# Feature weights loaded first through GpSimd's queue, with K and Q alone on the two hardware queues

## The chip, the cores and the metric

The kernel runs on one core of a Trainium2 chip. The metric is device time in microseconds of one execution. A core has five engines with lists of their own: TensorE (PE; its weight loads are listed apart as PEld), VectorE (DVE), ScalarE (ACT), GpSimd (POOL) and SyncE (SP). Three of them issue transfers here, each on its own queue: SP and ScalarE on hardware queues, GpSimd on a queue whose transfers can also change the number type. 16 DMA engines carry all of them.

## The reference

Two layers follow each other. The first is linear attention with a feature map: K and Q, 8 batches of 8 heads of 576 tokens of 64 numbers, are multiplied by one 64 x 128 matrix `w_phi`, and the features are exponentials of the result and of its negative.

```python
def phi(x):
    proj = np.einsum('bhsd,df->bhsf', x, w_phi)
    proj = proj - np.max(np.abs(proj), axis=-1, keepdims=True)
    return np.concatenate([np.exp(proj), np.exp(-proj)], axis=-1)
q_p, k_p = (phi(q), phi(k))
kv = np.einsum('bhsf,bhsd->bhfd', k_p, v)
z = np.sum(k_p, axis=2)
num = np.einsum('bhsf,bhfd->bhsd', q_p, kv)
den = np.einsum('bhsf,bhf->bhs', q_p, z)[..., None] + 1e-06
return (num / den).astype(np.float32)
```

The second takes the heads side by side as 512 channels, forms a gate by a causal convolution over 5 tokens and a sigmoid, multiplies it with `x @ w_val`, and multiplies by `w_out`. The result is 8 x 576 x 512 in float32.

## The kernel before

The work is cut into 40 units. Units 0 to 31 hold two heads each (four units to a batch) and eight of each token group's nine tokens; units 32 to 39 hold the ninth tokens of a batch. For each unit TensorE transposes K and Q (step T), a copy brings the transposes to SBUF (C), TensorE multiplies them with the weights (PK for K by token, PA and PQ for Q), VectorE takes maxima (MA, MB, MQ), ScalarE takes exponentials (KA, KB, XA, XB), GpSimd scales V (V), and TensorE forms kv (KV) and the output (N). The second layer follows batch by batch (GF, TH, VA, VB, GV, OA, OB, OE, ST).

The order of all this is a list written out by hand, `ORDER` (lines 31 to 108). A token names a step, its unit, after @ the PSUM banks, and after a colon the engine. Each engine and each queue carries out its part in this order; where data come from another engine or a transfer it waits, and all that stands behind it on the same engine waits too.

Ahead of the list stands an opening that the list doesn't govern (lines 157 to 238). GpSimd makes the identity `ident_bf` (line 158). The first two heads of K and of Q come in float32 to the staging buffers `first["k"]` and `first["q"]` (shown as GV, whose memory they borrow), half through SP's queue and half through ScalarE's (lines 189 and 195). The weights come to `wtmp` twice, to the upper and the lower 64 partitions (line 193), between K and Q on the same two queues. VectorE clears buffers and derives a negative identity and two small ones from `ident_bf` (lines 203 to 233). Everything else of K, Q and V comes through GpSimd's queue, which changes it to bf16 on the way, by the steps LD of the list.

The list then begins like this:

```python
LD.0 LD.1 CQ.0:D Z.1:P CK.0:A T.0@5 LD.3 LD.2 W.0:A C.0:A PK.0@0,2 KA.0 TX.0@7 CX.0:A MB.0 T.1@1 C.1:D
PA.0@6,7 PK.1@1,3 KB.0 KB.1 PQ.0@2,4 MQ.0 MA.1 SA.0 MB.1 KA.1 MA.0 T.2@5 C.2:D T.3@3 XA.0 WB.0:P C.3:D
T.32@0,1 C.32:D PA.3@6,7 XB.0 LD.4 PK.32@0,1 E.0 LD.6 LD.7 LD.5 FL.6@4 PK.2@5,2:W K0.32 K1.32 MQ.3 MB.2 KA.2
```

CK.0 and CQ.0 cast the first K (ScalarE) and Q (VectorE) to bf16. T.0 transposes that K and TX.0 that Q, C.0 and CX.0 copy the transposes, both on ScalarE. W.0 casts the weights to `W2` on ScalarE, between CK.0 and C.0; WB.0 casts them to the zero-padded `W2Z` on GpSimd. LD.0 and LD.1 load heads 2 and 3 of batch 0 of K and Q, which T.1 reads; LD.2 and LD.3 load its other four heads, which T.2 and T.3 read. LD.4 and LD.5 load V of batch 0, LD.6 and LD.7 K and Q of batch 1, the first reader of which is T.4.

Of the kernel before, what the change touches and what calls it, by code (L numbers as in the profile page):

```python
# [10 lines left out]
ALU = mybir.AluOpType  # L11
AX = mybir.AxisListType

FP32 = mybir.dt.float32
# [3 lines left out]
F = 128  # L18
DM = 512
P = 128  # L20
# [95 lines left out]
def kernel(  # L116
# [11 lines left out]
    nc = tc.nc  # L128
    ctx.enter_context(nc.allow_low_precision("bf16 operands of the matmuls"))

    def pool(name, bufs):
        return ctx.enter_context(tc.tile_pool(name=name, bufs=bufs))

    const = pool("const", 1)
# [19 lines left out]

    ctx.enter_context(tc.manual_schedule())

    ident_bf = const.tile([P, P], BF16, name="ident_bf")
    make_identity(nc, ident_bf[:])

# [28 lines left out]
        first[name] = first[name].rearrange("p (a j d) -> p a j d", a=1, d=D)  # L188
    main_dma((nc.sync, nc.scalar), "k", 0, 0, 1, first["k"])
    W2 = const.tile([P, F], BF16, name="W2")  # L190
    wtmp = const.tile([P, F], FP32, name="wtmp")
    for t in range(2):
        (nc.sync, nc.scalar)[t].dma_start(wtmp[t * 64:(t + 1) * 64, :], w_phi[:, :])
    for t in range(2):
        (nc.sync, nc.scalar)[t].dma_start(
            first["q"][t * 64:(t + 1) * 64, 0, :, :].rearrange("p j d -> p (j d)"),
# [4 lines left out]
    nident = const.tile([P, P], BF16, name="nident")  # L201
# [3 lines left out]
    nc.scalar.activation(warm[:, :], zero[:, 0:1], AF.Exp)  # L205
    W2Z = const.tile([P, 2, F], BF16, name="W2Z")
    nc.vector.memset(W2Z[:, :, :].rearrange("p a f -> p (a f)"), 0.0)
    nc.vector.tensor_scalar_mul(nident[:, :], ident_bf[:, :], -1.0)
    ident5 = const.tile([5, 5], FP32, name="ident5")
    nc.vector.tensor_copy(ident5[:, :], ident_bf[0:5, 0:5])  # L210
    id32 = const.tile([P, 32], FP32, name="id32")
    nc.vector.tensor_tensor(id32[:, :], ident_bf[:, 0:32], ident_bf[:, 32:64], ALU.add)
    nc.vector.tensor_tensor(id32[:, :], id32[:, :], ident_bf[:, 64:96], ALU.add)
    nc.vector.tensor_tensor(id32[:, :], id32[:, :], ident_bf[:, 96:128], ALU.add)

    XTs = []
    for i in range(2):
        t = const.tile([P, HP, (4 + J) * 64], BF16, name=f"XT{i}")
# [12 lines left out]
    MQA = const.tile([P, 40, 4, 2], BF16, name="MQA")  # L231
    MQX = const.tile([P, NG, P], BF16, name="MQX")
    nc.vector.memset(MQX[:, :, :].rearrange("p g c -> p (g c)"), 0.0)
    MQT = const.tile([P, NG, P], BF16, name="MQT")
    EA = const.tile([P, 40, 2, 4, 2], FP32, name="EA")
    RCPA = const.tile([P, 40, 8], FP32, name="RCPA")
# [3 lines left out]
    def copy(eng, dst, x, bank=()):  # L240
        if eng == "A":
            read(nc.scalar.activation(dst, x, AF.Copy), bank)  # L242
        else:
            read(engines[eng].tensor_copy(dst, x), bank)  # L244
# [317 lines left out]
    def op_MC(i, eng):  # L562
        x, bank = units[i].MT
        copy(eng, MQT[:, i // G % NG, :], x, bank)

# [91 lines left out]
    def op_SA(i):  # L657
        u = units[i]
        for blk in range(2 if u.tail else 4):
            for par in range(2):  # L660
# [3 lines left out]
                else:  # L664
                    r = slice(par * 64, par * 64 + 64)
                    c = par * 64 + i % G * 4 + blk
                    lhs, rhs = nident[r, c:c + 1].to_broadcast([64, P]), MQT[r, i // G % NG, :]
                nc.tensor.matmul(cols, lhs, rhs, start=False, stop=True, skip_group_check=True)  # L668
# [260 lines left out]
    for token in ORDER.split():  # L929
        head, _, eng = token.partition(":")  # L930
        head, _, bank = head.partition("@")
        name, _, idx = head.partition(".")
# [39 lines left out]
```

## Time and profile before

| | us |
|---|---|
| median of 3 runs | 225.01 |
| lowest and highest | 224.21, 226.33 |
| the profiled execution's own time | 226.87 |
| its span, first to last instruction | 225.1 |
| transfers of GpSimd's queue (q0), share of the 16 DMA engines' span | 47.6% |

In the profile a row of the timeline gives the start in us, the duration, the engine, the line, the operation, what it writes and reads, and in brackets the engine's idle time before it and what ended that. A row of transfers gives what is loaded, the queue that issues it, its size and the microseconds from issue to landing. Line numbers are those of the kernel before; line 178 issues K and V, 172 Q on GpSimd's queue, 193 the weights, 195 the first Q; 242 and 244 are the helper `copy` on ScalarE and on the other engines; 393 is a transpose and 443 a product with the weights.

### The profile page before, as it was taken

The numbers are of one execution on the slowest core, as the hardware profiler recorded it, in microseconds if no ns is written. First come the engines' busy times: TensorE is split into PE (matmuls) and PEld (weight loads), VectorE is DVE, ScalarE is ACT, GpSimd is POOL, SyncE is SP. The second block draws the span as 40 slices with busy tenths as digits, with TensorE's granted clock in tenths as the row PEclk, the third lists the DMA queues.
The fourth block names the chain that finished last, engine by engine and source line by source line (L and its number), as shares of the span: only waits on it lengthen the run. The fifth ranks groups of instructions, "written<-read, shape, count | busy, mean of one in ns | idle before, by whom it ended". The sixth has DMA issues, their size and how long they took to land.

```text
span 225.1 us, 8971 instructions
## 1 busy us (share of the span) xinstructions
PE 202.4 (90%) x3828; PEld 138.2 (61%) x3854; DVE 184.1 (82%) x337; ACT 194.4 (86%) x425; POOL 133.4 (59%) x172
## 2 busy tenths in 40 slices
PE   0687899996798999999998999999999999999997
PEld 0464677765465665678656775776676666466542
DVE  6499999987886999889996999999988997466341
ACT  3599999998988998999998999999989998777541
POOL 8779967999779702993359509952816086500100
PEclk9997999999999999999999999999999999999999
DMA  5999997699999996984928595796550226304846
GB/s 114 197 199 218 270 203 116 121 204 173 132 167 205 152 147 142 179 141 55 197 50 115 62 203 111 169 136 111 126 114 20 57 47 129 134 4 114 247 105 192
DMA packets 41362, 31.38 MB, mean 139 GB/s; under 512 B 16869, under 2 KB 37349, under 8 KB 41322
## 3 DMA queue, kind: packets, MB, share of 16 engines
q0 software_dynamic: 20816, 14.90, 47.6%
q1 hardware_dynamic: 19882, 15.04, 29.9%
q10 hardware_dynamic: 624, 0.87, 1.2%
q8 instruction: 30, 0.49, 0.9%
q14 instruction: 10, 0.08, 0.1%
HBM read 32.58 MB, written 9.44 MB: 187 GB/s over the span
## 4 chain that ended last, share of the span: by engine, by line
PE 57%; ACT 26%; DVE 9%; issue 3%; DMA 2%; SPq 1%; ACTq 0%; DVEq 0%
PE PS L841 11%; PE PS L812 10%; ACT QT L551 9%; ACT KT L538 8%; PE PS L443 5%; PE PS L706 5%; PE PS L629 4%; PE PS L393 4%; ACT GATE L801 3%; PE PS L652 3%; PE PS L785 3%; PE PS L668 2%; DMA GV<-in_q_dram 2%; DVE MKA L509 2%; PE PS L288 2%
## 5 line engine op out<-in xcount | busy, mean ns | idle before, releaser
L615 POOL TENSOR_TENSOR VT<-vN,EA 128x1024 bf16<-128x1024 bf16 x32 | 61.0, 1907 | 37.2 <-ACT EA L569 30.8
L538 ACT ACTIVATE KT<-PS 128x512 bf16<-128x512 f32 x128 | 70.7, 659 | 2.3 <-PE PS L443 2.2
L551 ACT ACTIVATE QT<-PS 128x512 bf16<-128x512 f32 x128 | 69.2, 657 | 2.8 <-PE PS L668 2.5
L509 DVE TENSOR_REDUCE MKA<-PS 128x4 f32<-128x512 f32 x64 | 42.6, 682 | 1.6 <-ACT KT L538 0.8
L494 DVE TENSOR_REDUCE MQX<-PS 128x8 bf16<-128x1024 f32 x30 | 36.5, 1219 | 4.7 <-PE PS L443 4.4
L812 PE MATMUL PS<-XT,WVAL 128*128 128x512 bf16 x128 | 34.8, 380 | 0.1
L841 PE MATMUL PS<-WOUT,GV 128*128 128x512 bf16 x107 | 30.9, 380 | 1.3 <-issue 0.6
L443 PE MATMUL PS<-W,T 64*128 64x128 bf16 x472 | 24.5, 223 | 4.3 <-ACT T L242 1.8
L828 DVE SCALAR_TENSOR_TENSOR GV<-GATE,PS 128x512 bf16<-128x512 bf16 x32 | 20.9, 680 | 5.3 <-PE PS L812 5.3
L443 PEld LDWEIGHTS <-T 64*128 64x128 bf16 x472 | 15.9, 96 | 12.9 <-issue 6.6
L726 DVE TENSOR_TENSOR XN<-PS,RCPA 128x512 bf16<-128x512 f32 x32 | 22.1, 692 | 1.1
L606 POOL TENSOR_TENSOR VTZ<-vN,EA 64x512 bf16<-64x512 bf16 x16 | 16.6, 1040 | 10.3 <-PE PS L668 6.5
L629 PEld LDWEIGHTS <-KT 128*128 128x128 bf16 x512 | 18.6, 97 | 6.6 <-ACT QT L551 1.2
L629 PE MATMUL PS<-VT,KT 128*128 128x65 bf16 x512 | 21.0, 193 | 1.5 <-ACT QT L551 0.6
L244 POOL COPY XT<-XT 128x1008 bf16<-128x1008 bf16 x8 | 8.2, 1025 | 22.3 <-ACT XT L242 16.1
L706 PEld LDWEIGHTS <-QT 128*128 128x128 bf16 x512 | 18.6, 97 | 4.3 <-issue 0.4
L706 PE MATMUL PS<-KVSA,QT 128*128 128x65 bf16 x512 | 20.6, 193 | 0.1
L244 DVE COPY T<-PS 128x1024 bf16<-128x1024 bf16 x27 | 18.3, 683 | 1.6 <-PE PS L393 1.6
L393 PE MATMUL PS<-ident_bf,kN 128*128 128x128 bf16 x128 | 13.5, 233 | 6.1 <-ACT kN L242 5.5
L801 ACT ACTIVATE GATE<-PS 128x1024 bf16<-128x1024 f32 x16 | 16.0, 1082 | 3.4 <-PE PS L785 3.4
L812 PEld LDWEIGHTS <-WVAL 128*128 128x128 bf16 x128 | 10.5, 97 | 8.4 <-issue 0.6
L852 DVE TENSOR_SCALAR OS<-PS 128x512 f32<-128x512 f32 x16 | 10.9, 685 | 5.5 <-PE PS L841 5.5
(103 smaller groups left out, 371.1 us busy)
## 6 DMA issues: line engine op xcount, KB each, us to landing
out_dram<-OS SPq DMA_DIRECT2D x28, 256.0 KB, 3.6
kN<-in_k_dram POOLq DMA_DIRECT2D x14, 320.0 KB, 7.1
vN<-in_v_dram POOLq DMA_DIRECT2D x14, 320.0 KB, 5.9
qN<-in_q_dram POOLq DMA_DIRECT2D x7, 576.0 KB, 10.8
OS<-in_moe_w_val_dram SPq DMA_DIRECT2D x1, 1024.0 KB, 9.4
out_dram<-OSt SPq DMA_DIRECT2D x8, 128.0 KB, 2.4
vN<-in_v_dram POOLq DMA_DIRECT2D x4, 160.0 KB, 8.0
OS<-in_moe_w_out_dram SPq DMA_DIRECT2D x2, 256.0 KB, 4.4
```

The costliest lines, as they stand in the source:

```text
L244: read(engines[eng].tensor_copy(dst, x), bank)
L443: nc.tensor.matmul(PS[:, bank[par], c0 + blk * P:c0 + (blk + 1) * P], u.T[r, i, blk, :], W2[r, :], start=True, stop=True,)
L494: read(nc.vector.tensor_reduce(MQX[:, i // G % NG, :].rearrange("p (r c) -> p r c", r=2)[:, :, c:c + 4], tokview(u.PA, 0, u, None), AX.X, ...
L509: read(nc.vector.tensor_reduce(out, half_ps(bank, x, out, wide), AX.X, ALU.max, apply_absolute_value=True,), [bank[x]])
L538: read(nc.scalar.activation(out, half_ps(u.PK, x, out, u.PKwide), AF.Exp, scale=1.0 if ft == 0 else -1.0,), [u.PK[x]])
L551: read(nc.scalar.activation(dst, PS[:, u.PQ[x], :].rearrange("p (x t) -> p x t", t=64), AF.Exp, scale=1.0 if ft == 0 else -1.0,), [u.PQ[x]])
L615: e.tensor_tensor(u.VT[:, :, :, 0:D], x.unsqueeze(1).to_broadcast([P, 2, n, D]), w.unsqueeze(3).to_broadcast([P, 2, n, D]), ALU.mult,)
L629: nc.tensor.matmul(PS[:, bank[0], c:c + E1], u.KT[:, ft, j // 2, j % 2, :], u.VT[:, ft, j, :], start=(jj == 0 and x == 0), stop=False, ski ...
L706: nc.tensor.matmul(PS[:, bank[c // 2], x * E1:(x + 1) * E1], u.QT[:, ft, c, h2, :, :].rearrange("p j t -> p (j t)"), kv[:, ft, h2, :], sta ...
L801: read(nc.scalar.activation(m.GATE[q2][:, :, :], banks(*bank), AF.Tanh), bank)
L812: nc.tensor.matmul(PS[:, m.val[jt], :], WVAL[:, dt, jt * P:(jt + 1) * P], planes(xt(m.b), slice(0, P), dt, 4), start=(dt == 0), stop=(dt = ...
L841: nc.tensor.matmul(PS[:, bank, :], lhs(jt), WOUT[:, jt, :], start=(jt == 0), stop=(jt == 3))
```

## The change

The two transfers of the weights leave SP's and ScalarE's queues, and are issued by GpSimd ahead of the identity. The five instructions of VectorE that read the identity move behind its clears. The hand-written list is the same.

```diff
     ctx.enter_context(tc.manual_schedule())
 
+    wtmp = const.tile([P, F], FP32, name="wtmp")
+    for t in range(2):
+        nc.gpsimd.dma_start(wtmp[t * 64:(t + 1) * 64, :], w_phi[:, :])
     ident_bf = const.tile([P, P], BF16, name="ident_bf")
     make_identity(nc, ident_bf[:])
...
     W2 = const.tile([P, F], BF16, name="W2")
-    wtmp = const.tile([P, F], FP32, name="wtmp")
-    for t in range(2):
-        (nc.sync, nc.scalar)[t].dma_start(wtmp[t * 64:(t + 1) * 64, :], w_phi[:, :])
     for t in range(2):
         (nc.sync, nc.scalar)[t].dma_start(
...
     nc.vector.memset(W2Z[:, :, :].rearrange("p a f -> p (a f)"), 0.0)
-    nc.vector.tensor_scalar_mul(nident[:, :], ident_bf[:, :], -1.0)
-    ident5 = const.tile([5, 5], FP32, name="ident5")
-    nc.vector.tensor_copy(ident5[:, :], ident_bf[0:5, 0:5])
-    id32 = const.tile([P, 32], FP32, name="id32")
-    nc.vector.tensor_tensor(id32[:, :], ident_bf[:, 0:32], ident_bf[:, 32:64], ALU.add)
-    nc.vector.tensor_tensor(id32[:, :], id32[:, :], ident_bf[:, 64:96], ALU.add)
-    nc.vector.tensor_tensor(id32[:, :], id32[:, :], ident_bf[:, 96:128], ALU.add)
...
     nc.vector.memset(MQX[:, :, :].rearrange("p g c -> p (g c)"), 0.0)
+    nc.vector.tensor_scalar_mul(nident[:, :], ident_bf[:, :], -1.0)
+    ident5 = const.tile([5, 5], FP32, name="ident5")
+    nc.vector.tensor_copy(ident5[:, :], ident_bf[0:5, 0:5])
+    id32 = const.tile([P, 32], FP32, name="id32")
+    nc.vector.tensor_tensor(id32[:, :], ident_bf[:, 0:32], ident_bf[:, 32:64], ALU.add)
+    nc.vector.tensor_tensor(id32[:, :], id32[:, :], ident_bf[:, 64:96], ALU.add)
+    nc.vector.tensor_tensor(id32[:, :], id32[:, :], ident_bf[:, 96:128], ALU.add)
```

GpSimd's list before, from the identity to the first load of V. The rows at lines 178 and 172 are LD.0, LD.1, LD.3 and LD.2, then come the two casts of WB.0 and LD.4; DMASW and DMAHW are semaphores of transfers of GpSimd's and of the hardware queues:

```order
masks.py:197 MEMSET ident_bf 128x128
masks.py:199 ISA
masks.py:199 AFFINE_SELECT ident_bf<-ident_bf 128x128 [waits Pool_49]
L178 DMA kN<-in_k_dram 64x2x320 x2
L172 DMA qN<-in_q_dram 128x576
L334 MEMSET OS 128x1
L172 DMA qN<-in_q_dram 128x2x576
L178 DMA kN<-in_k_dram 64x4x320 x2
L244 CAST W2Z<-wtmp 64x128 [waits DMAHW3_49,DVE_49]
L244 CAST W2Z<-wtmp 64x128 [waits DMAHW2_49,Pool_49]
L178 DMA vN<-in_v_dram 64x4x320 x2
```

The same place now (the line numbers of the changed kernel are a few higher or lower):

```order
L159 DMA wtmp<-in_w_phi_dram 64x128 x2
masks.py:197 MEMSET ident_bf 128x128
masks.py:199 ISA
masks.py:199 AFFINE_SELECT ident_bf<-ident_bf 128x128 [waits Pool_49]
L181 DMA kN<-in_k_dram 64x2x320 x2
L175 DMA qN<-in_q_dram 128x576
L333 MEMSET OS 128x1
L175 DMA qN<-in_q_dram 128x2x576
L181 DMA kN<-in_k_dram 64x4x320 x2
L243 CAST W2Z<-wtmp 64x128 [waits DMASW0_49,DVE_49]
L243 CAST W2Z<-wtmp 64x128 [waits DMASW1_49,Pool_49]
L181 DMA vN<-in_v_dram 64x4x320 x2
```

Two issues stand ahead of the identity and of every load of this queue, and the casts of WB.0 wait for transfers of the same queue. The order behind is the same.

ScalarE's list before, from its first issue to C.0 (the third row is the issue of the first Q, the last four are CK.0, W.0, C.0 and the first exponential):

```order
L178 DMA GV<-in_k_dram 64x2x320
L193 DMA wtmp<-in_w_phi_dram 64x128
L195 DMA GV<-in_q_dram 64x576
L205 ACT_TABLE_LOAD
L205 ACTIVATE warm<-zero 128x1 [waits DVE_49]
L242 ACTIVATE kN<-GV 128x640 [waits DMAHW1_49,DMAHW0_49]
L242 ACTIVATE W_109<-wtmp 128x128 [waits DMAHW3_49,DMAHW2_49]
L242 ACTIVATE T<-PS 128x512 [waits PE_49]
L538 ACTIVATE KT<-PS 128x4x128 [waits PE_49]
```

The same place now:

```order
L181 DMA GV<-in_k_dram 64x2x320
L195 DMA GV<-in_q_dram 64x576
L205 ACT_TABLE_LOAD
L205 ACTIVATE warm<-zero 128x1 [waits DVE_49]
L241 ACTIVATE kN<-GV 128x640 [waits DMAHW1_49,DMAHW0_49]
L241 ACTIVATE W_112<-wtmp 128x128 [waits DMASW1_49,DMASW0_49]
L241 ACTIVATE T<-PS 128x512 [waits PE_49]
L537 ACTIVATE KT<-PS 128x4x128 [waits PE_49]
```

One issue less stands between K and Q (SP's list loses the same row), and W.0 waits for GpSimd's queue.

VectorE's list before, from the second clear to CQ.0 (XT, DIAGF, VTZ and MQX are clears):

```order
L207 MEMSET W2Z 128x128
L208 TENSOR_SCALAR nident<-ident_bf 128x128 [waits Pool_49]
L210 CAST ident_124<-ident_bf 5x5
L212 TENSOR_TENSOR id_126<-ident_bf 128x32
L213 TENSOR_TENSOR id_126<-id_126,ident_bf 128x32 [waits DVE_49]
L214 TENSOR_TENSOR id_126<-id_126,ident_bf 128x32 [waits DVE_49]
L219 MEMSET XT_130 128x4x4
L219 MEMSET XT_132 128x4x4
L227 MEMSET DIAGF 128x1280
L229 MEMSET VTZ_140 128x1040
L233 MEMSET MQX 128x256
L244 CAST qN<-GV 128x576 [waits DMAHW5_49,DMAHW4_49]
```

The same place now:

```order
L207 MEMSET W2Z 128x128
L211 MEMSET XT_123 128x4x4
L211 MEMSET XT_125 128x4x4
L219 MEMSET DIAGF 128x1280
L221 MEMSET VTZ_133 128x1040
L225 MEMSET MQX 128x256
L226 TENSOR_SCALAR nident<-ident_bf 128x128 [waits Pool_49]
L228 CAST ident_141<-ident_bf 5x5
L230 TENSOR_TENSOR id_143<-ident_bf 128x32
L231 TENSOR_TENSOR id_143<-id_143,ident_bf 128x32 [waits DVE_49]
L232 TENSOR_TENSOR id_143<-id_143,ident_bf 128x32 [waits DVE_49]
L243 CAST qN<-GV 128x576 [waits DMAHW3_49,DMAHW2_49]
```

The wait for the identity stands behind all clears, and CQ.0 still comes behind the same twelve instructions.

## The prediction

> **What bounds the kernel now.** I read the page first, then the chain of work that ended last in order of time, then the timeline of the first 14 us, and last the transfers issued in short windows of it.
>
> ```profile
> span 225.1 us, 8971 instructions
> PE 202.4 (90%) x3828; PEld 138.2 (61%) x3854; DVE 184.1 (82%) x337; ACT 194.4 (86%) x425; POOL 133.4 (59%) x172
> PE 57%; ACT 26%; DVE 9%; issue 3%; DMA 2%; SPq 1%; ACTq 0%; DVEq 0%
> ...
> 2.42 5.33 DMA GV<-in_q_dram
> 8.37 1.48 PE PS L393 x12
> 9.87 0.70 DVE T L244
> ```
>
> TensorE, ScalarE and VectorE are each busy over 80% of the span, and the chain is compute from 8.37 us to the end. Only its head is a transfer: the 5.33 us in which the first head pair of Q came in. What the change can move directly is therefore the opening, and what it gains there lasts only if no later transfer gives it back. The opening, with the start in us first, then the duration, and the idle time of the engine and its releaser in brackets:
>
> ```profile
> 1.44 1.37 POOL L178 DMA_DIRECT2D kN<-in_k_dram  x2
> 2.80 0.58 POOL L172 DMA_DIRECT2D qN<-in_q_dram  x1
> 3.41 0.73 POOL L172 DMA_DIRECT2D qN<-in_q_dram  x1
> 4.11 1.28 POOL L178 DMA_DIRECT2D kN<-in_k_dram  x2
> 4.67 0.74 ACT L242 ACTIVATE kN<-GV 128x640 bf16<-128x640 f32 x1 [0.38 <-DMA GV<-in_k_dram]
> 5.46 0.61 PE L393 MATMUL PS<-ident_bf,kN 128*128 128x128 bf16 x4 [5.46 <-ACT kN L242]
> 6.71 0.31 ACT L242 ACTIVATE W<-wtmp 128x128 bf16<-128x128 f32 x1 [1.30 <-DMA wtmp<-in_w_phi_dram]
> 6.76 0.63 POOL L244 CAST W2Z<-wtmp 64x128 bf16<-64x128 f32 x2 [1.37 <-DMA wtmp<-in_w_phi_dram]
> 6.92 0.58 ACT L242 ACTIVATE T<-PS 128x512 bf16<-128x512 bf16 x1
> 7.34 1.24 POOL L178 DMA_DIRECT2D vN<-in_v_dram  x2
> 7.55 0.61 PE L443 MATMUL PS<-W,T 64*128 64x128 bf16 x8 [1.49 <-ACT T L242]
> 7.85 0.46 DVE L244 CAST qN<-GV 128x576 bf16<-128x576 f32 x1 [2.88 <-DMA GV<-in_q_dram]
> 8.66 0.47 PEld L393 LDWEIGHTS <-kN 128*128 128x128 bf16 x4
> 9.09 0.47 PEld L393 LDWEIGHTS <-qN 128*128 128x128 bf16 x4
> 9.17 0.61 ACT L242 ACTIVATE T<-PS 128x512 bf16<-128x512 bf16 x1
> 9.82 0.34 PEld L443 LDWEIGHTS <-T 64*128 64x128 bf16 x8 [0.26 <-ACT T L242]
> 9.89 0.82 POOL L172 DMA_DIRECT2D qN<-in_q_dram  x1
> 10.48 1.23 DVE L478 TENSOR_REDUCE MQA<-PS 128x8 bf16<-128x1024 f32 x1
> 12.48 0.47 PEld L393 LDWEIGHTS <-kN 128*128 128x128 bf16 x4
> 21.03 0.47 PEld L393 LDWEIGHTS <-qN 128*128 128x128 bf16 x4
> ```
>
> Two waits for transfers stand here. ScalarE casts the feature weights (W.0, 6.71) after 1.30 us idle, and the copy behind it (C.0, 6.92) has been ready since TensorE ended T.0 at 5.46 + 0.61 = 6.07. VectorE casts Q (CQ.0, 7.85) after 2.88 us idle. The rows at 8.66 and 9.09 are T.1, the first step that reads the loads of GpSimd's queue; 12.48 is T.2; 21.03 is the Q half of T.4. When each transfer landed follows from rows of short windows (the last figure is us from issue to landing; the first row is what all queues moved in 40 slices of 12 us):
>
> ```profile
> GB/s 0 0 0 0 0 0 0 60 124 260 391 304 201 185 76 86 119 188 174 189 201 245 246 192 209 192 165 201 198 206 199 193 192 192 179 181 192 188 179 188
> GV<-in_k_dram SPq DMA_DIRECT2D x1, 160.0 KB, 3.8
> GV<-in_k_dram ACTq DMA_DIRECT2D x1, 160.0 KB, 3.2
> GV<-in_q_dram ACTq DMA_DIRECT2D x1, 144.0 KB, 5.4
> GV<-in_q_dram SPq DMA_DIRECT2D x1, 144.0 KB, 5.3
> wtmp<-in_w_phi_dram ACTq DMA_DIRECT2D x1, 32.0 KB, 3.4
> wtmp<-in_w_phi_dram SPq DMA_DIRECT2D x1, 32.0 KB, 5.1
> ...
> kN<-in_k_dram POOLq DMA_DIRECT2D x1, 80.0 KB, 3.6
> kN<-in_k_dram POOLq DMA_DIRECT2D x1, 80.0 KB, 5.9
> qN<-in_q_dram POOLq DMA_DIRECT2D x1, 144.0 KB, 5.8
> qN<-in_q_dram POOLq DMA_DIRECT2D x1, 288.0 KB, 6.6
> kN<-in_k_dram POOLq DMA_DIRECT2D x1, 160.0 KB, 6.9
> qN<-in_q_dram POOLq DMA_DIRECT2D x1, 576.0 KB, 10.8
> ```
>
> On GpSimd's queue the two pieces of LD.0 landed at 1.44 + 3.6 = 5.0 and about 2.1 + 5.9 = 8.0 (the second is issued half way through the 1.37 us), LD.1 at 2.80 + 5.8 = 8.6, LD.3 at 3.41 + 6.6 = 10.0, the last of LD.2 at about 4.75 + 6.9 = 11.65, and LD.7 at 9.89 + 10.8 = 20.7. The rate falls to 76 and 86 GB/s near 4.2 to 4.8 us, just where the weights' small pieces pass the two hardware queues, and is about 190 once GpSimd's queue runs alone.
>
> **The change part by part.**
>
> Added on GpSimd: two weight issues ahead of everything. No row has this transfer on this queue. The nearest is the pair of LD.0, also from 64 partitions: 1.37 us. The bounds are two of the shortest issue (2 x 0.58 = 1.16) and two of the longest (2 x 0.82 = 1.64). I take 1.37. The identity and LD.0, LD.1, LD.3, LD.2 all move back by that. TensorE first needs the identity at 5.46, so that part is free. The loads' issue now ends at 4.11 + 1.28 + 1.37 = 6.76, and GpSimd stood idle 1.37 us before its casts at 6.76, so from there its list, with LD.4 at 7.34 and all later loads, stays where it was. The cost of this part is only that four early loads are issued 1.37 us later; it falls on T.1 and T.2, below.
>
> Where the weights land: issued at about 0.74 and 1.4, where SP and ScalarE issue K now. With 3.6 us (LD.0's first piece, alone at the head of this queue, as the weights will be) the second lands at 5.0; with 5.9 at 7.3. Before, the later half landed at 1.55 + 5.1 = 6.65. I take 5.0, by the row whose place in the queue is the same. ScalarE is ready for W.0 at 4.67 + 0.74 = 5.41, so its 1.30 us of waiting goes.
>
> Removed on SP and ScalarE: the weights' issues, behind K and ahead of Q. K keeps its issue; beside it 64 KB of weights now run on a third queue instead of behind it. Bounds for K's later half: from 0.6 earlier (the other half landed 3.2 after issue, not 3.8) to 0.2 later (64 KB at the 304 to 391 GB/s of K's own slices). I take no move, so CK.0 stays at 4.67.
>
> ScalarE's path then is: CK.0 to 5.41, W.0 to 5.72 inside TensorE's T.0, and C.0 once T.0 ends: 6.07, plus 0.08 of handover, makes 6.15 instead of 6.92. That is **0.77 us**, and PK.0 (7.55), CX.0 (9.17), PA.0 (9.82) and the reduction MQ.0 (10.48) hang on it one after another.
>
> Q: its two issues come earlier by the removed ones, to about 1.5 us on both queues. With the same 5.4 us to landing Q is there at 6.9 instead of 7.7, and CQ.0 starts at about 7.0 instead of 7.85: 0.85 us, a little more than the other path, and so no bound. If Q were as fast as K it would be there at 5.3, and nothing more would come of that, since TX.0 stands behind PK.0 in TensorE's list.
>
> The clears: the same twelve instructions of VectorE in another order; the five on the identity go last, which keeps VectorE from waiting for an identity that is now 1.37 us later. VectorE was done with all of them 2.88 us before CQ.0. If that cover were gone they would cost what the identity is late, 1.37 us at most. Taken as nothing.
>
> What is late next: T.1 now wants LD.0 at 8.66 - 0.77 = 7.89 and LD.1 at 9.09 - 0.77 = 8.32. They are issued at up to 3.5 and at 4.17. With 3.6 us they land at 7.1 and 7.8, with the old 5.9 and 5.8 at 9.4 and 10.0. I expect near the short end: the old long times are those of loads that shared the engines with the weights and Q on the hardware queues, which are now largely through by 6.9. Alone, the queue moved LD.2's 320 KB between 10.0 and 11.65, 194 KB/us, so LD.0's second 80 KB and LD.1's 144 KB need 1.2 us after the first piece, 2.81 + 3.6 = 6.4: LD.1 at 7.6, or 7.9 with some of Q still beside it. That just holds, and puts the queue some 0.7 us ahead. T.2 then wants its K by 12.48 - 0.77 = 11.71, which even the old 11.65 meets, and T.4 wants LD.7 by 21.03 - 0.77 = 20.26, where the old 20.7 less 0.7 gives 20.0.
>
> [...]
>
> Sum: -0.77 on the path that sets the end, all else covered. Against the profiled execution that is a span of 225.1 - 0.77 = 224.3. That execution's own time was 226.87, 1.8 above its span, and the median of the three runs is 225.01, 1.86 below it. I subtract from the median, since the opening is the same in every run: 225.01 - 0.77 = **224.2 us**.
>
> **The rivals.**
>
> *The queue does not catch up.* LD.1 lands at 8.6 and LD.7 at 20.7 as before, since the same bytes pass the same engines. Then T.1 and above all T.4 wait, and the gain is the slack that T.4 had: 21.03 - 20.7 = 0.33. Time 224.7. For it: from about 6 us on the engines move a steady 190 GB/s. Against: the trough of 76 GB/s should go.
>
> *GpSimd's loads become the wait* (slower). If LD.1 keeps its 5.8 us from issue, it lands at 10.0 and T.1's Q half starts 0.9 later than its 9.09, with VectorE's copy behind it and everything after: 225.01 + 0.9 = 225.9. It decides once LD.1 lands after 9.09. Weights that land at 7.3 instead of 6.65 cost about 0.65 by the same kind of lateness.
>
> *K gains too.* With the hardware queues to itself K's later half lands like the earlier one, 0.6 sooner, and CK.0 with it: 0.77 + 0.6 = 1.37, and T.1 then stands on LD.1. Time 223.6.
>
> *The clock.* One stretch ran at half clock:
>
> ```profile
> 20.10:23.50 3.40, 3.40 (x38) 2.51 (x35) 2.79 (x5) 3.40 (x10) 3.34 (x7) 0.53 1.25 257
> ```
>
> After the window's ends and length stand busy time and count of PE, PEld, DVE, ACT and POOL, then the granted clock, the DMA share and GB/s. TensorE is busy all 3.40 us at a clock of 0.53 and VectorE idles 0.61. If the shift moves TensorE's thin spots so that this stretch goes, 0.61 more is won (223.6); if a second one comes, the gain is gone (224.9). [...]
>
> **How the numbers follow.** Chances: the forecast 0.42; the queue not catching up 0.22; GpSimd's loads as the wait 0.13; K gaining too 0.12; the clock, either way, 0.11. The last two reach down to 223.6, the slow rival up to 225.9. The three runs of before lie 0.8 below and 1.3 above their median, and a median of the changed kernel is open by about half of that, so I put the range at 223.2 to 225.9. A measurement of this kernel tells some 1% (2.25 us) from no change, and no case but a sum of several reaches that: faster by over 1% means below 222.76 (0.06), slower above 227.26 (0.04), within 0.90.
>
> **What would show it.** The steps hold if ScalarE casts the weights right behind K with no idle time; if C.0 starts near 6.15 and PK.0 near 6.8; if Q is cast near 7.0; if GpSimd goes from LD.2 to its casts without a gap and issues LD.4 near 7.3; if T.1 waits for no transfer; and if T.4 starts 0.7 us earlier. The prediction is wrong if T.1 or T.4 shows a wait on GpSimd's queue, if the weights land after 5.4, or if K's cast starts after 4.9.

## The result, and the profile after

The changed kernel took 226.71 us at the median of 20 runs (224.07 to 227.82), the kernel before 224.99 (223.51 to 228.04, also 20 runs beside them). The ratio is 1.0067, with a 95% interval of 1.0039 to 1.0094: 1.5 us slower by that ratio, where 0.8 us of gain was forecast, and above 225.9, the upper end of the forecast range. A second session, below, gave 1.0034 [1.0003, 1.0064].

The page of the changed kernel, its span, the engines and the shares of the chain:

```profile
span 224.3 us, 8995 instructions
PE 203.6 (91%) x3854; PEld 137.7 (61%) x3854; DVE 183.9 (82%) x337; ACT 194.1 (87%) x425; POOL 134.6 (60%) x174
PE 54%; ACT 17%; DVE 14%; DMA 7%; POOL 3%; issue 3%; ACTq 0%; POOLq 0%
```

The chain in order of time (start, length, what), its head and its longest piece:

```profile
3.09 1.15 POOL kN L181 x2
4.25 4.21 DMA qN<-in_q_dram
...
52.49 10.39 DMA kN<-in_k_dram
```

The span of this pair of profiles fell by 0.8 us, from 225.1 to 224.3, which is just the span forecast, while the timed medians went the other way. That agreement is luck: a profile shows one execution, this one took 226.09, less than its median, and that of before, 226.87, lay 1.9 above its own. The chain says more. Its head was the first Q on a hardware queue (2.42, 5.33 us). Now it is GpSimd's issue of LD.0 and the landing of LD.1, and in the middle it hangs for 10.39 us on the K of batch 3. Transfers went from 2% of the chain to 7%, GpSimd from nothing shown to 3%.

The timeline of the opening after, in the same form as before:

```profile
1.26 1.25 POOL L159 DMA_DIRECT2D wtmp<-in_w_phi_dram  x2 [0.81 <-POOLq L955]
3.04 1.24 POOL L181 DMA_DIRECT2D kN<-in_k_dram  x2
5.55 1.29 POOL L181 DMA_DIRECT2D kN<-in_k_dram  x2
5.73 0.31 ACT L241 ACTIVATE W<-wtmp 128x128 bf16<-128x128 f32 x1 [0.37 <-DMA wtmp<-in_w_phi_dram]
6.05 0.60 ACT L241 ACTIVATE T<-PS 128x512 bf16<-128x512 bf16 x1
6.08 0.46 DVE L243 CAST qN<-GV 128x576 bf16<-128x576 f32 x1 [1.24 <-DMA GV<-in_q_dram]
6.71 0.61 PE L442 MATMUL PS<-W,T 64*128 64x128 bf16 x8 [0.69 <-ACT T L241]
6.79 0.71 POOL L243 CAST W2Z<-wtmp 64x128 bf16<-64x128 f32 x2
7.44 1.24 POOL L181 DMA_DIRECT2D vN<-in_v_dram  x2
7.65 0.63 PE L392 MATMUL PS<-ident_bf,kN 128*128 128x128 bf16 x4
8.49 0.61 PE L392 MATMUL PS<-ident_bf,qN 128*128 128x128 bf16 x4 [0.21 <-DMA qN<-in_q_dram]
11.96 0.59 PE L392 MATMUL PS<-ident_bf,kN 128*128 128x128 bf16 x4
```

The hoped-for part is there: the weights cost ScalarE 0.37 us instead of 1.30, C.0 starts at 6.05, PK.0 at 6.71, Q is cast at 6.08, T.1 starts at 7.65 instead of 8.77. Then part of it melts: T.1's Q half waits 0.21 us for LD.1, and at T.2 (11.96, before 12.59) 0.63 us is left of 1.12. In this pair 0.72 us of lead still stands at T.4 (20.73, 20.01); in the repeats below it does not.

The profiles of two experiments below, issue_only and after_q6late_b, fell in disturbed executions (mean clock 0.978 and 0.985), so their marks behind T.4 and their spans are left out.

### The profile page after: what moved, and what is told of

The parts are those of the page before. It is cut to its first block, busy times and chain, and to the rows that moved or that the text cites. A ratio compares the mean times of both kernels' runs of the same rounds, so it can differ in the third digit from the quotient of the medians.

```text
span 224.3 us, 8995 instructions
## 1 busy us (share of the span) xinstructions
PE 203.6 (91%) x3854; PEld 137.7 (61%) x3854; DVE 183.9 (82%) x337; ACT 194.1 (87%) x425; POOL 134.6 (60%) x174
## 4 chain that ended last, share of the span: by engine, by line
PE 54%; ACT 17%; DVE 14%; DMA 7%; POOL 3%; issue 3%; ACTq 0%; POOLq 0%
PE PS L840 12%; PE PS L811 9%; ACT QT L550 7%; DMA kN<-in_k_dram 5%; PE PS L705 5%; ACT KT L537 4%; PE PS L442 4%; PE PS L392 4%; DVE MQX L493 4%; PE PS L628 4%; DVE MKA L508 3%; PE PS L784 3%; PE PS L667 3%; ACT GATE L800 3%; PE PS L651 3%
## 5 line engine op out<-in xcount | busy, mean ns | idle before, releaser
L550 ACT ACTIVATE QT<-PS 128x512 bf16<-128x512 f32 x128 | 69.9, 679 | 2.4 <-PE PS L667 2.2
L840 PE MATMUL PS<-WOUT,GV 128*128 128x512 bf16 x128 | 35.0, 380 | 0.1
L392 PEld LDWEIGHTS <-kN 128*128 128x128 bf16 x128 | 9.4, 102 | 12.1 <-ACT kN L241 5.4
```

The costliest lines, as they stand in the source:

```text
L392: nc.tensor.transpose(u.Tps[:, x, blk, :], a, ident_bf[:, :])
L550: read(nc.scalar.activation(dst, PS[:, u.PQ[x], :].rearrange("p (x t) -> p x t", t=64), AF.Exp, scale=1.0 if ft == 0 else -1.0,), [u.PQ[x]])
L840: nc.tensor.matmul(PS[:, bank, :], lhs(jt), WOUT[:, jt, :], start=(jt == 0), stop=(jt == 3))
```

## The experiments

Each kernel ran in five rounds beside the kernel before. "q6late" marks a kernel in which LD.22 (Q of batch 6) moves in the list from its place ahead of KM.1 to the place behind LD.21, for a reason given below. The table has one profile of each: when PK.0 starts, when T.1 and T.2 start (with TensorE's wait for a transfer ahead of T.2), when the last piece of LD.2 lands, when T.4 and T.13 start, and the span. The last column is the timed ratio to the kernel before.

| kernel | PK.0 | T.1 | LD.2 lands | T.2 (wait) | T.4 | T.13 | span | ratio [95%] |
|---|---|---|---|---|---|---|---|---|
| before (first profile) | 7.55 | 8.77 | 11.65 | 12.59 | 20.73 | 64.18 | 225.1 | |
| before_again | 6.95 | 8.35 | 11.66 | 11.98 | 19.93 | 62.57 | 223.6 | 0.9983 [0.9952, 1.0014] |
| clears_only | 6.79 | 8.55 | 11.64 | 12.36 | 20.20 | 61.52 | 222.6 | 1.0042 [1.0015, 1.0069] |
| before_q6late | 6.95 | 8.94 | 11.76 | 12.75 | 20.57 | 61.27 | 222.8 | 0.9973 [0.9948, 0.9998] |
| before_q6late_b | 7.36 | 9.81 | 12.39 | 13.62 | 21.39 | 62.09 | 223.1 | 0.9944 [0.9917, 0.9970] |
| after (first profile) | 6.71 | 7.65 | 11.83 | 11.96 | 20.01 | 63.02 | 224.3 | 1.0067 [1.0039, 1.0094] |
| after_again | 6.62 | 7.57 | 12.65 | 12.79 (0.92) | 21.45 | 62.61 | 224.2 | 1.0034 [1.0003, 1.0064] |
| dma_only | 6.63 | 7.59 | 13.08 | 13.21 (1.17) | 21.88 | 62.81 | 223.9 | 1.0011 [0.9977, 1.0046] |
| after_q6late | 6.97 | 7.92 | 12.95 | 13.08 (0.41) | 21.43 | 62.13 | 223.8 | 0.9972 [0.9941, 1.0003] |
| after_q6late_b | 6.82 | 7.76 | 11.95 | 12.09 | 19.90 | - | - | 0.9965 [0.9928, 1.0002] |
| issue_only | 6.99 | 8.12 | 12.73 | 13.01 | 20.86 | - | - | 1.0013 [0.9983, 1.0044] |
| issue_q6late | 6.69 | 8.03 | 12.33 | 12.47 | 20.82 | 61.53 | 223.2 | 1.0003 [0.9969, 1.0038] |
| no_w | 6.53 | 7.58 | 10.91 | 11.56 | 19.81 | 62.40 | 223.8 | 0.9947 [0.9913, 0.9980] |
| no_w_q6late | 6.77 | 7.71 | 10.87 | 11.81 | 20.21 | 60.91 | 222.5 | 0.9939 [0.9913, 0.9965] |
| w_one | 9.37 | 10.31 | 12.89 | 14.40 | 22.24 | 63.51 | 225.5 | 1.0058 [1.0022, 1.0094] |
| w_one_q6late | 8.75 | 9.70 | 12.22 | 13.79 | 21.63 | 62.91 | 224.4 | 1.0007 [0.9974, 1.0039] |
| q_first | 8.10 | 9.04 | 10.92 | 13.13 | 21.31 | 64.25 | 225.1 | 1.0038 [1.0008, 1.0068] |
| q_first_q6late | 8.32 | 9.26 | 11.41 | 13.35 | 21.45 | 62.15 | 224.6 | 0.9997 [0.9968, 1.0025] |

### Both kernels again, and the two halves of the change

before_again and after_again are the two kernels unchanged. dma_only moves the weights to GpSimd and leaves VectorE's order; clears_only does the reverse:

```diff
 # clears_only, against the kernel before
     nc.vector.memset(W2Z[:, :, :].rearrange("p a f -> p (a f)"), 0.0)
-    nc.vector.tensor_scalar_mul(nident[:, :], ident_bf[:, :], -1.0)
...
     nc.vector.memset(MQX[:, :, :].rearrange("p g c -> p (g c)"), 0.0)
+    nc.vector.tensor_scalar_mul(nident[:, :], ident_bf[:, :], -1.0)
```

> The kernel of before once more, unchanged, for a second profile and a measure of the noise: ratio 1.000, within 0.004. Theory 1 (transfers in the middle): most executions of before are near 225.0, 1.9 below its first profile, so this profile should have no half-clock stretch, and the K load of batch 3 that T.12 reads should land by about 61.5 instead of 62.1, with T.12 starting near 62. Theory 2 (the clock alone): everything from 24 us on stands about 1.2 earlier than in the first profile, and the transfers are where they were.

> The changed kernel once more. All theories: ratio 1.004 to 1.009, T.1 near 8.5 and MQ.0 near 9.75. Theory 1: TensorE waits 1 to 3 us for the K load of batch 3 ahead of T.12 (landing near 62.9). Theory 2: no such wait in this profile, or a half-clock stretch in it.

> Only the weights' transfers move to GpSimd's queue; VectorE's five instructions on the identity stay ahead of its clears. Theory 1: VectorE waits for the identity until about 3.1 us and is done with its clears near 6.5, just beyond Q's landing near 6.0, so CQ.0 starts some 0.4 later than in the changed kernel, PK.0 not at all; ratio as that of the whole change, 1.004 to 1.009. Theory 3 (the order of the clears carries the loss): ratio 1.000 or below.

> Only the order of VectorE's opening changes; the weights stay on the hardware queues between K and Q. Theory 1: VectorE waits 2.9 us for Q in either order, so ratio 1.000 within 0.004. Theory 3 (the order of the clears carries the loss): 1.004 to 1.009.

The repeats did not do what was expected of them in the middle: after_again has no wait for K of batch 3. The repeat of the kernel before showed first how unusual its first profile had been:

```profile
6.10 0.31 ACT L242 ACTIVATE W<-wtmp 128x128 bf16<-128x128 f32 x1 [0.71 <-DMA wtmp<-in_w_phi_dram]
6.95 0.61 PE L443 MATMUL PS<-W,T 64*128 64x128 bf16 x8 [0.90 <-ACT T L242]
7.43 0.46 DVE L244 CAST qN<-GV 128x576 bf16<-128x576 f32 x1 [2.45 <-DMA GV<-in_q_dram]
7.95 0.61 PE L393 MATMUL PS<-ident_bf,qN 128*128 128x128 bf16 x4 [0.39 <-DVE qN L244]
8.35 0.63 PE L393 MATMUL PS<-ident_bf,kN 128*128 128x128 bf16 x4
11.98 0.39 PE L393 MATMUL PS<-ident_bf,kN 128*128 128x128 bf16 x4
```

ScalarE waits 0.71 us for the weights, not 1.30, and PK.0 starts at 6.95, not 7.55. What holds T.1 is the row at 7.95: TX.0 waits 0.39 us for the cast of Q (0.76 in clears_only, 0.98 in before_q6late, 1.44 in before_q6late_b).

The repeats with the weights on GpSimd showed the price. These are the first rows of T.2 in after_again, dma_only and after_q6late, in this order:

```profile
12.79 0.58 PE L392 MATMUL PS<-ident_bf,kN 128*128 128x128 bf16 x4 [0.92 <-DMA kN<-in_k_dram]
```

```profile
13.21 0.59 PE L392 MATMUL PS<-ident_bf,kN 128*128 128x128 bf16 x4 [1.17 <-DMA kN<-in_k_dram]
```

```profile
13.08 0.58 PE L392 MATMUL PS<-ident_bf,kN 128*128 128x128 bf16 x4 [0.41 <-DMA kN<-in_k_dram]
```

TensorE waits for LD.2. These are three of the five profiles with the weights first on GpSimd's queue; the other two, and all with the early loads at their old place, don't have this wait. In clears_only LD.2 lands at 11.64 as before and T.2 does not wait, so the clears are not its cause.

The times do not divide in the same way. By them alone the order of the clears costs (1.0042, inside the 1.004 to 1.009 that this rival gave) and the transfers cost little (dma_only, 1.0011, below the range that the first theory gave, though its interval reaches into it). The trace of clears_only can't settle it: it shows no new wait, but the profiled execution was the fastest of its twelve (224.38, median 226.16). The rival stays open.

The rate of the transfers between 6 and 11 us shows why LD.2 is late. The rows give, after the stretch, the busy time and count of PE, PEld, DVE, ACT and POOL, the clock, the DMA share and GB/s; before_again first, then after_again:

```profile
6.00:11.00 5.00, 3.47 (x39) 2.33 (x38) 2.61 (x4) 3.50 (x8) 4.58 (x8) 1.00 1.23 187
```

```profile
6.00:11.00 5.00, 3.78 (x40) 2.53 (x41) 3.30 (x5) 4.02 (x8) 4.86 (x9) 1.00 1.08 142
```

The five profiles with the weights on the hardware queues and no dummies moved 168 to 199 GB/s in this stretch, the five of the changed placement 135 to 161. The means, 183 and 146, differ by 37 GB/s; over 5 us that is 185 KB, 1.0 us at 183 GB/s. In the changed placement Q is through at 6.0 to 6.4 us, and what is left is what GpSimd has issued; issued 1.6 us later, it moves at the lower rate. Where the loads stay at their old place and Q is through nearly as early (no_w and its twin, below, at 6.0 to 6.6), the rate is 180; where only the issue is late (issue_only and its twin) it is 152 and 160. Why the rate is lower is not shown.

### Moving LD.22: where the middle hides the opening

After 41 us the two kernels' paths had been 1.7 us apart (T.9 at 39.63 in before_again, 41.34 in after_again), and at T.13 only 0.04. T.9 and T.13 are the transposes of units 9 and 13; unit 13 is of batch 3. In the first profile after, T.13 waits for a transfer:

```profile
63.02 0.38 PE L392 MATMUL PS<-ident_bf,kN 128*128 128x128 bf16 x4 [2.16 <-DMA kN<-in_k_dram]
```

It is K of batch 3. GpSimd issues it behind its copy of XT, and the copy needs four transposes that SyncE's queue carries; the last of them lands at 42.99 to 44.60 in the profiles of the two kernels and their halves (here at 43.68, and the copy starts at 43.97).

In the two repeats, though, T.13 waits for no transfer: K has landed 0.5 and 0.7 us before it. The lead of before_again goes into two idle times of TensorE. The profile puts the first down to a copy by ScalarE and names nothing for the second; in after_again they are 0.08 and 0.24. First before_again, then T.13 of after_again:

```profile
52.12 0.23 PE L560 MATMUL PS<-ident_bf,MQX 128*128 128x128 bf16 x1 [1.34 <-ACT KVSA L242]
60.33 0.46 PE L443 MATMUL PS<-W,T 64*128 64x128 bf16 x10 [0.94 <-issue]
62.57 0.39 PE L393 MATMUL PS<-ident_bf,kN 128*128 128x128 bf16 x4
```

```profile
62.61 0.39 PE L392 MATMUL PS<-ident_bf,kN 128*128 128x128 bf16 x4
```

Moving LD.22 out of the transposes' way takes both kinds off:

```diff
-... KV.1@1 KV.0@7 LD.22 KM.1:D V.3:P LW.0 KM.0:D
+... KV.1@1 KV.0@7 KM.1:D V.3:P LW.0 KM.0:D
...
-... E.18 LD.21 V.17:P V.19:P
+... E.18 LD.21 LD.22 V.17:P V.19:P
```

> Kernel before, with one load moved: Q of batch 6 (LD.22, 576 KB, issued near 26 us though first read after 120 us) goes behind K of batch 6 (LD.21). Theory 1 (the kernel stands on transfers between 43 and 62 us, so that an opening gained is lost there): the transposes of unit 3 land by 42 instead of 43.0 to 43.7, the K load of batch 3 by 59 to 60 instead of 61.4 to 62.1, T.13 starts near 60 to 61 instead of 61.5 to 64.2, ratio 0.985 to 0.995. Rival (the middle is compute, and the transfers are just in time): T.13 near 62.5, ratio 1.000.

> The changed kernel with the same load moved. Theory 1: with the stand in the middle gone, the time follows the opening, so it is to the kernel before with the load moved as T.3's end is in the two profiles: equal where T.2 waits for nothing, up to 0.8 us slower where T.2 waits for LD.2; ratio 0.985 to 0.997. Rival (the loss of the changed kernel lies behind 62 us): ratio 1.004 to 1.009 above that of the kernel before with the load moved, and more than 160.7 us from T.12 to the end.

The fourth transpose landed at 40.92 and 41.71 instead of 42.99 to 44.60, and T.13 waits for nothing. In all eight profiles with LD.22 moved, these and those below, T.9 to T.13 takes 21.00 or 21.01 us whatever the opening was. With LD.22 in place it takes 21.0 to 21.3 in four of the profiles in the table (clears_only, dma_only, after_again, w_one) and 22.9 to 23.4 in five: with the wait for K in after and no_w, with the two idle times in before, before_again and q_first. So the middle can take up to 2.4 us, but does not always, and why the move also ends the idle times is not shown.

With LD.22 moved the opening's difference goes through: 0.86 us at T.4 (20.57, 21.43), 0.86 at T.9, 0.86 at T.13 (61.27, 62.13), 1.0 in the span. The timed medians, 224.95 and 225.09, do not tell the two apart, and the gain over the kernel before, 0.9973, is less than the 0.985 to 0.995 expected.

### Cost alone, and gain alone

issue_only leaves the weights on the hardware queues and puts two unread transfers of them first on GpSimd's queue. no_w leaves the transfer of the weights out; `wtmp` is the constant 0.01, so that its output is that of other weights.

```diff
 # issue_only, against the kernel before
+    wdum = const.tile([P, F], FP32, name="wdum")
+    for t in range(2):
+        nc.gpsimd.dma_start(wdum[t * 64:(t + 1) * 64, :], w_phi[:, :])
...
 # no_w, against the kernel before
-    for t in range(2):
-        (nc.sync, nc.scalar)[t].dma_start(wtmp[t * 64:(t + 1) * 64, :], w_phi[:, :])
...
+    nc.vector.memset(wtmp[:, :], 0.01)
```

> Kernel before, with two more transfers of the weights issued by GpSimd ahead of its identity into a tile that nothing reads; the kernel's own weights stay on the hardware queues. This is the cost of the change without its gain: LD.0 to LD.2 are issued 1.5 us later. If GpSimd's early loads are what is lost: LD.2 lands at 12.8 to 13.3 instead of 11.65, T.2 starts that late and waits 0.8 us or more, ratio 1.003 to 1.008. If the stand in the middle swallows what is lost before it, as it does what is gained: T.2 waits, but T.13 stays at 62 to 63, and the ratio is 1.000 within 0.003.

> Kernel before without the transfers of the weights: they are a constant set by VectorE, so the output differs from the reference. This is the gain of the change without its cost: no weights between K and Q, and GpSimd's loads are issued when they were. C.0 near 6.1, PK.0 near 6.7, T.2 near 11.7 just at LD.2's landing. If the opening's gain lasts: T.13 0.3 to 0.8 us earlier, ratio 0.996 to 0.999. If the stand in the middle swallows it: T.13 at 61.5 to 62.6 and a ratio of 1.000 within 0.003.

> The kernel before with LD.22 moved (so that T.13 does not stand on a late K) and two unread weight transfers first on GpSimd's queue; the weights that are read stay on the two hardware queues. Theory 'later issue': the four early loads of GpSimd's queue are issued 1.6 us later with no gain beside it, so PK.0 stays near 6.95, LD.2 lands near 12.7 to 13.2 (11.76 without the dummies), T.2 waits for it and starts near 13.0 to 13.9, T.4 near 21.3 to 21.9, T.13 near 62.0 to 62.7 (61.27 without), with no wait there; the span is about 1 us above 222.8 and the time 1.001 to 1.007 of before. Rival 'bytes, not order': 64 KB more at some 190 KB/us are 0.34 us, so LD.2 lands at 12.1 at most and T.13 at 61.6 at most. Rival 'the placement of W is what costs, not the order of the loads': nothing moves, since W itself stays where it was.

> Leaves out the transfer of the weights; W is a constant written by VectorE. LD.22 moved. This is the gain of the change without its cost. Theory 'later issue': PK.0 near 6.5, LD.0 to LD.2 issued as before, LD.2 lands near 10.9, T.2 at 11.5 to 12.0 without a wait, T.4 19.6 to 20.0, T.13 near 60.3 to 60.8 without a wait, span near 222, time 0.991 to 0.996 of before, below the 0.9973 of the kernel before with the same move. Rival 'the middle gives it back in any case': T.13 at 61.3 or later, with a wait on K of batch 3, and the time at 0.997.

With the dummies LD.2 lands at 12.73 and 12.33, 1.1 and 0.6 later than in before_again and before_q6late, toward what the theory said (before_q6late_b has it at 12.39 without them); T.2 does not wait for it, against the theory. Here T.1 waits, in both halves, and the transfers of Q show something not expected (issue_q6late, the timeline and the issues, which end with the us to landing):

```profile
8.03 0.58 PE L396 MATMUL PS<-ident_bf,kN 128*128 128x128 bf16 x4 [0.19 <-DMA kN<-in_k_dram]
9.02 0.61 PE L396 MATMUL PS<-ident_bf,qN 128*128 128x128 bf16 x4 [0.40 <-DMA qN<-in_q_dram]
```

```profile
GV<-in_q_dram ACTq DMA_DIRECT2D x1, 144.0 KB, 4.1
GV<-in_q_dram SPq DMA_DIRECT2D x1, 144.0 KB, 4.0
```

Q stands behind the weights on its queues, as before, and yet lands 4.0 to 4.1 us after its issue (4.2 in issue_only) instead of 4.9 to 6.2. On the hardware queues nothing was changed, only GpSimd's loads come later (LD.0 at 3.04 in issue_q6late, 1.44 in the first profile before): Q gains where they lose. The gain of the change at T.1 and its loss at T.2 may thus be partly one trade between two queues; it is not shown, and w_one below, where the loads come late too (LD.0 at 2.80), has Q 6.4 to 6.6 us after its issue. At T.4 the dummies cost 0.25 us (20.57, 20.82), at T.13 0.26 (61.27, 61.53), less than the 0.7 to 1.4 expected; the time, 1.0003, lies above both twins without them (0.9973, 0.9944), the intervals overlapping with the first and just touching the second.

Without any transfer of the weights the kernel is faster, 0.9947 and 0.9939, the first by more than either theory gave it. LD.2 lands at 10.9, T.2 starts at 11.56 and 11.81 with no wait. So the gain is real where nobody pays for it. But of 1.2 us at T.1 (8.94 to 7.71) only 0.36 arrives at T.13 (61.27 to 60.91), against an expected 60.3 to 60.8. Of the 0.87 that goes missing 0.58 lies between T.2 and T.4 (7.82, 8.40), where TensorE waits for no transfer: there its pace rose later (near 15.4 us, against 13.6), as the last section shows. And no_w, with LD.22 in place and 1.24 us of waiting for K at T.13, timed as fast as its twin; the profiled execution, 225.56, lay 0.9 above its median, so it may not be typical.

### Other places for the weights

w_one sends the weights as one transfer to 128 partitions, q_first leaves them on the hardware queues but behind Q.

```diff
 # w_one, against the changed kernel
-    for t in range(2):
-        nc.gpsimd.dma_start(wtmp[t * 64:(t + 1) * 64, :], w_phi[:, :])
+    nc.gpsimd.dma_start(wtmp[:, :], w_phi.unsqueeze(0).broadcast_to([2, 64, F]))
```

> The changed kernel, LD.22 in its place, weights as one transfer on GpSimd's queue. Theory 'later issue': LD.2 lands near 12.2, T.2 at 12.2 to 12.4 with little wait, T.4 20.4 to 20.7, T.13 between 61.9 and 62.9 since it stands on K of batch 3; time 0.998 to 1.003. Rival 'bytes and packets first': as the changed kernel, T.2 with a wait of 0.4 or more in most profiles, T.4 at 21.4, time 1.003 to 1.007.

> The changed kernel with LD.22 moved and the weights as one transfer to 128 partitions (the 64 rows read twice) in place of two, first on GpSimd's queue. Theory 'later issue': one issue of about 0.65 in place of two, so LD.0 is issued near 2.4 instead of 3.04 and LD.2's last piece lands near 12.2 to 12.4 (12.95 with two, 11.76 with none); T.2 waits 0 to 0.2 and starts near 12.3, T.4 near 20.6, T.13 near 61.3; PK.0 6.6 to 6.9. Span 222.8 to 223.2, time 0.995 to 0.999. Rival 'any transfer ahead of them on the queue costs the same, since its bytes and packets go first': LD.2 lands at 12.9 or later, T.2 at 13.0 or later, T.13 at 62.1.

> The kernel before with LD.22 moved and, on the two hardware queues, Q ahead of the weights; GpSimd's queue as before. Theory 'Q's landing is what sets T.1 before, and GpSimd's early loads must not be delayed': Q lands near 6.2 in place of 7.2 to 7.8, the weights near 6.2 to 6.6, PK.0 at 6.9 to 7.3, no wait of TX.0 for the cast of Q, T.1 at 7.9 to 8.3, LD.2 still at 11.7, T.2 without a wait near 12.0, T.13 near 60.8; time 0.994 to 0.997. Rival 'the small pieces of the weights slow whatever they run beside, in either order': Q no earlier than 7.0 or the weights at 7.5 or later, T.1 at 8.5 or later and the time as the twin without the swap.

> The kernel before with Q ahead of the weights on the hardware queues, LD.22 in its place. Theory: T.1 at 7.9 to 8.3 and T.2 near 12.0 as in the run with LD.22 moved, T.13 between 61.5 and 62.5 since it stands on K of batch 3; time 0.996 to 1.001. Rival: as the kernel before, T.1 at 8.4 to 8.9, time 0.998 to 1.002.

Both fail, each at the weights. The rows are the weights' cast and their transfers, first of w_one, then of q_first_q6late:

```profile
8.52 0.31 ACT L240 ACTIVATE W<-wtmp 128x128 bf16<-128x128 f32 x1 [3.06 <-DMA wtmp<-in_w_phi_dram]
```

```profile
wtmp<-in_w_phi_dram POOLq DMA_DIRECT2D x1, 64.0 KB, 7.2
```

```profile
7.47 0.31 ACT L242 ACTIVATE W<-wtmp 128x128 bf16<-128x128 f32 x1 [2.25 <-DMA wtmp<-in_w_phi_dram]
```

```profile
wtmp<-in_w_phi_dram SPq DMA_DIRECT2D x1, 32.0 KB, 5.1
wtmp<-in_w_phi_dram ACTq DMA_DIRECT2D x1, 32.0 KB, 5.0
```

One transfer of 64 KB needs 7.2 us (6.6 in the twin) where two of 32 KB need 3.6 each, and its single issue took 1.00 us, so that LD.0 moved forward by only 0.24 (3.04 to 2.80): w_one says little of a shorter issue. LD.2 landed at 12.22 in the twin, as the theory of the later issue had it, and at 12.89 in w_one, nearer the rival's value; T.2 came 1.5 to 1.6 us after it in both, held up by the weights. Behind Q the weights land 5.0 us after their issue, PK.0 starts at 8.1 to 8.3, and the bound passes from Q to the weights; Q itself landed at 6.0 and 7.0 instead of 7.3 to 8.6, and it did not help. So each place had its price: with the weights ahead of Q, Q landed at 7.3 to 8.6; with them behind Q, PK.0 starts at 8.1 to 8.3; with two transfers of them first on GpSimd's queue, LD.2 lands at 11.83 to 13.08, in the mean of five profiles 0.7 us later.

The pair with LD.22 moved ran once more on one chip:

> The kernel before with LD.22 moved, once more, beside its changed twin on one chip. Theory 'the loss of the opening reaches the end where no late K of batch 3 hides it': T.1 at 8.3 to 8.9, T.2 12.0 to 12.8, TensorE's transposes at 0.10 us each from about 13.5 us on, T.4 near 20.2, T.13 near 61.0 without a wait; time 0.995 to 0.999 of before, and 0.002 to 0.005 below its changed twin of this call. Rival 'the pair is level': both within 0.0015 of each other.

> The changed kernel with LD.22 moved, once more. Theory 'the loss reaches the end': T.1 near 7.6 to 7.9, T.2 at 12.6 to 13.2 with 0.3 to 1.2 us of waiting on LD.2, transposes at 0.155 us each through T.3 and at 0.10 only from 16 us on, T.4 at 21.2 to 21.9, T.13 near 62.0; time 0.998 to 1.003, above its twin by 0.002 to 0.005. Rival 'the pair is level': both within 0.0015 of each other.

The ratios, 0.9944 and 0.9965, differ in the expected direction by 0.2%, within their intervals. The traces miss the expectation in both directions: before_q6late_b had the latest opening of its kind (Q cast at 8.68, T.1 at 9.81) and the shorter time nonetheless, and in after_q6late_b the opening held to T.4 at 19.90. There the next load was the wait, LD.7 (0.66 us before T.4's Q half), and TensorE's granted clock was 0.50 from 20.0 to 26.4 us (last section).

before_q6late beats both kernels of the case: 0.9973 [0.9948, 0.9998] and 0.9944 [0.9917, 0.9970].

## Why the prediction was wrong

**The step that failed** is the one on GpSimd's queue: that its loads, issued 1.37 us later, would land near the short end, "some 0.7 us ahead", and that T.2's need at 11.71 would be met by "even the old 11.65". LD.2 was issued 1.44 us later (5.55 for 4.11) and landed at 11.83, 12.65, 13.08, 12.95 and 11.95 in the five profiles. The step took 194 KB/us for the queue alone from a stretch at 10 to 11.65 us and applied it from 6.4 us on; between 6 and 11 us 135 to 161 GB/s were measured. So the second rival, GpSimd's loads as the wait, is what came in three of the five, at T.2 rather than at T.1 where its point of decision had been put; the 0.2 to 0.6 us of waiting at T.1's Q half, in three of the five, are only its beginning. In the mean of five profiles of each placement T.1 starts 1.2 us earlier (8.88, 7.70), LD.2 lands 0.7 later (11.82, 12.49), and T.2 starts level (12.66, 12.63): the gain is used up there.

**The gain** was there, but its working used the wrong rows. The -0.77 us for W was sized from one execution in which the weights landed at 6.62; the other four of that placement had them at 5.9 to 6.4. Their PK.0 starts at 7.01 in the mean, that of the five changed ones at 6.75: 0.26 us. Q's path, called "no bound", was the bound at T.1 in every repeat. T.1 gained 0.78 us between the repeats (8.35, 7.57) and 1.02 between before_q6late and after_q6late. The forecast was subtracted from the median "since the opening is the same in every run"; in the five profiles of the old placement T.1 starts anywhere from 8.35 to 9.81.

**GpSimd's issue** was taken as 1.37 us. The two issues took 1.25, but the first began only at 1.26 where the identity's fill had begun at 0.74, and LD.0 moved by 1.60 (1.44 to 3.04). The cover of 1.37 us in front of its casts of W2Z was that execution's late weights, too: LD.4 stood at 6.73 in before_again and at 7.44 after. So the later loads did not stay where they were: LD.7 landed at 20.43 to 21.64 instead of 19.45 to 20.70, where 20.0 had been reckoned.

**W, C.0, CQ.0, K** came near what was expected: the weights' last piece at 5.5 to 5.9 (5.0 taken, so that ScalarE still waited 0.37 us), C.0 at 6.05, 0.03 behind T.0's end at 6.02 (6.15, with a handover of 0.08 by the author's estimate), Q cast at 6.08 to 6.68 (7.0), K's cast unmoved. The clears cost nothing that a trace shows, but their timed 1.0042 is open.

**The opening's gain lasting to the end** was assumed. From T.9 to T.13 it holds, for a gain and a loss alike, in the eight profiles with LD.22 moved; in the kernel as it stands that stretch takes 0 to 2.4 us more, by a wait for K of batch 3 or by idle times of TensorE. How the timed 0.3 to 0.7%, 0.8 to 1.5 us, comes about is therefore not settled. At T.4 the changed placement is 0.9 to 1.7 us behind in three of the five pairs of profiles and 0.7 and 1.5 ahead in the other two, 20.93 against 20.56 in the mean. That the hoped-for gain is gone by T.2 is shown; what makes the kernel slower than before is not.

**The clock rival** named a half-speed stretch that goes or comes, and its size was about right: from T.4 to T.9 the four profiles with one such stretch (before, clears_only, w_one and its twin) take 20.0 to 20.3 us, those without 19.7 to 19.9. It came and went in both placements and does not explain the difference: clears_only had one and the second shortest span. That TensorE's thin spots bring it was the author's assumption, and it is not shown: from 17 to 19 us TensorE is busy 0.78 us in before, where the stretch follows, and 0.79 us in no_w_q6late, where none does. What was missed is TensorE's pace in the opening. T.2 to T.4 takes 7.8 us in the seven profiles in which the pace rises during T.2 or T.3, and 8.05 to 8.67 in the nine in which it rises after T.3. (The two others are the kernel before's: 8.14 in the first, with the half-speed stretch ahead of T.4, and 7.95 in the second, where the pace had risen ahead of T.2.) Four of the five profiles of the changed placement are among the nine and none of the old. That part of the loss, some 0.3 to 0.9 us, comes on top of the wait for LD.2; but both kernels without the weights' transfer, where T.2 waits for nothing, are among the nine as well, so the wait is not needed for it.

## What to carry to other kernels

A transfer put first on a queue was paid for here by the loads behind it (LD.2 landed 0.7 us later in the mean of five profiles): look up when the last of them is needed, and take the rate it will run at from a stretch in which that queue stood in the same company (194 KB/us was taken, 135 to 161 GB/s measured). The short waits in this opening varied from execution to execution by as much as they are long (in the old placement ScalarE's for the weights was 1.30 and 0.71 us, TX.0's for the cast of Q 0.21 to 1.44), so size such a wait from several profiles. Before counting on an early gain or fearing an early loss, find the next place at which the kernel stands on something that the opening doesn't move. Cutting the span at marks, as at T.2, T.4, T.9 and T.13 here, shows in which stretch two executions part.

## What was not expected of the hardware

In the opening TensorE runs slow and speeds up at one moment, while the profile's granted clock, in both kernels shown here, reads 1.00 in every stretch from 6 to 20 us. These are rows of before_q6late, the transposes of T.2 and T.3 (four to a row), and below them of after_again:

```profile
12.75 0.63 PE L393 MATMUL PS<-ident_bf,kN 128*128 128x128 bf16 x4
13.17 0.61 PE L393 MATMUL PS<-ident_bf,qN 128*128 128x128 bf16 x4
13.60 0.41 PE L393 MATMUL PS<-ident_bf,kN 128*128 128x128 bf16 x4
13.85 0.39 PE L393 MATMUL PS<-ident_bf,qN 128*128 128x128 bf16 x4
```

```profile
13.16 0.63 PE L392 MATMUL PS<-ident_bf,qN 128*128 128x128 bf16 x4
14.02 0.63 PE L392 MATMUL PS<-ident_bf,qN 128*128 128x128 bf16 x4
15.44 0.61 PE L442 MATMUL PS<-W,T 64*128 64x128 bf16 x8 [0.42 <-DVE T L243]
18.51 0.40 PE L442 MATMUL PS<-W,T 64*128 64x128 bf16 x8
```

Four transposes take 0.58 to 0.63 us before the rise and 0.38 to 0.41 after; it came at about 13.6 us in the first kernel and between 17 and 18.5 in the second, where TensorE had waited 0.92 us ahead of T.2. The earliest rise seen was near 11.5 (before_again, where T.2 at 11.98 already takes 0.39 us for four). The half-speed stretch, unlike this rise, shows in the granted clock (clears_only, then after_q6late_b; the figure before the last two is the granted clock):

```profile
20.20:23.60 3.40, 3.40 (x35) 2.74 (x33) 3.12 (x6) 3.40 (x11) 3.34 (x7) 0.50 1.23 268
```

```profile
19.00:19.80 0.80, 0.60 (x11) 0.43 (x10) 0.80 (x4) 0.80 (x3) 0.80 (x2) 0.96 1.32 191
20.00:26.40 6.40, 5.74 (x57) 4.14 (x58) 4.57 (x8) 4.62 (x13) 4.44 (x8) 0.50 1.22 273
26.40:26.80 0.40, 0.40 (x6) 0.30 (x4) 0.40 (x1) 0.00 (x0) 0.40 (x1) 0.79 1.35 203
```

By the clocks of the rows on either side the second stretch ran from about 19.7 to 26.6 us, by estimate 6.8 us, where the one in clears_only has 3.40.

What sets the length of these stretches, and when the pace rises, no run here shows. That an idle stretch ahead of T.2 puts the rise off would fit after_again, but no run here tried it by itself, and no_w and no_w_q6late, without one, rise near 14.9 and 15.4 us.

Of the single transfer in w_one, 7.2 us for 64 KB (6.6 in the twin), the traces show the time and not the cause.
